# Top-k attention feeding two feed-forward layers: scores as float32 matmuls of 64 rows, the mask by a parametric relu, the gate by tanh, and one form of probabilities for all batches

## The chip, the core and the metric

The kernel runs on one core of a Trainium2 chip. The metric is the device time of one execution in microseconds; the kernel before takes 1081.91 us (median of three runs). The core has a matrix engine (PE, TensorE; PEld is its loading of the stationary operand), a vector engine (DVE), a scalar engine (ACT), a general engine (POOL) and a queue that starts DMA transfers (SP). Each engine works through its own list of instructions in order and waits at semaphores for the others.

## What is computed

Attention over 4 batches of 8 heads, 576 positions and 64 values a head, in which each row of scores keeps its 32 largest entries; its output, as 2304 rows of 512, goes through a gated layer (512 to 1536 to 512) and a layer with a softmax-weighted unit and a layer norm (512 to 1024 to 512).

```python
scores = scale * np.matmul(q, k.transpose(0, 1, 3, 2))
kth = np.partition(scores, -top_k, axis=-1)[..., -top_k:-top_k + 1]
scores = np.where(scores >= kth, scores, -1000000000.0)
attn = np.exp(scores - np.max(scores, axis=-1, keepdims=True))
attn = attn / (np.sum(attn, axis=-1, keepdims=True) + 1e-09)
x = np.matmul(attn, v)                      # then rows of 512
x = (1.0 / (1.0 + np.exp(-(x @ w_gate))) * (x @ w_val)) @ w_out
h = x @ w_in
solu = h * softmax(h)
ln = (solu - mean(solu)) / np.sqrt(var(solu) + 1e-06) * g_ln
return ln @ w_out2
```

## The kernel before

**Steps and chunks.** The attention runs in 72 steps. A step takes 128 query rows of two heads: 64 steps take a block of 128 queries and one pair of heads, eight take the last 64 queries of two pairs, stacked to 128 rows. Four steps fill a chunk of 128 output rows; there are 18 chunks, and each goes through the two layers a few steps after its attention.

**Scores of a step.** `split_k` (L606) and `rest_k` (L610) turn k of a head into a rounded half in partitions 0 to 63 and its rest in 64 to 127; `split_q` (L591) and `rest_q` (L595) do the same with q, which lies in both halves of the partitions. `scores` (L640) sums over 128 rows at once, two matmuls for each half of the 576 keys, in the format float32r. The PSUM tile `ps` has one buffer and holds the scores of one head, so a step goes through it twice: `take_scores` (ACT, L647) copies them to `s`, and `fold_max` and `fold_min` (DVE, L654 and L658) write the larger and the smaller of the two halves into `w`.

**Top 32.** Four rounds on DVE, `topk_max` (L668) with `topk_drop` (L672) in between, the first two over 288 columns and the rest over 576, give the eight largest at a time in `m8`.

**Mask and softmax.** `edge` and `edge_scale` (DVE, L686 and L690) make a scale from the 32nd value, `edge_bias` (POOL, L695 and L696) the bias; `below` (ACT, L701) takes a relu into `w`, which is zero for what stays and huge for what goes; `penal` (POOL, L705) subtracts it from `s`; `expo` (ACT, L710) takes the exponential and its sum; `total1` (POOL) and `inverse` (DVE, L719) give the factor.

**Probabilities.** In batch 0 (`WHOLE`) the row is scaled in float32 by `norm`, transposed on PE (`flip`, L736), copied from PSUM (`take_flip`, L743) and multiplied with float32 values. In the other batches the row becomes two float16 halves (`prob_hi` L749 on ACT, `norm` with one row on ACT at L725 and one on POOL at L727, `prob_lo` L753 on POOL), a DMA transposes them (L760), and `attend` (L779) takes three products of halves. `value_hi` and `value_lo` split v likewise.

**The layers.** `gate` and `value` (L934), `down` (L980), `hidden` (L1017) and `last` (L1115) run three products of float16 halves each. `sigmoid` (L959) takes the gate's twelve blocks in three instructions, after the twelfth; sigmoid and exponential lie in different function tables of ACT, so that a table load stands ahead of each change between them.

**Order.** `Order` is a planner written in Python that runs when the kernel is built. Each operation has an engine, a price in us, a rank, what it needs and which buffers it takes and gives back; the planner plays the five lists forward and emits the instructions in that order. `SHIFT` holds several hundred corrections to the ranks, and `BUFS` the number of buffers of each kind.

Of the kernel before, what the change touches and what calls it, by code (L numbers as in the profile page):

```python
# [43 lines left out]
FULL = 2.0 ** 15  # L44

BUFS = dict(s=3, ks=8, v=4, qr=3, qs=3, w=3, et=2, ps=1, pt=1, av=1, pm=4, xt=1, gh=1, two=3, big=2, xf=1, x2=1)
# [9 lines left out]
EARLY = 6  # L56

# [1201 lines left out]
```

## Time and profile before

| | |
|---|---|
| device time, median of three runs | 1081.91 us (1080.01 to 1081.96) |
| span of the profiled execution | 1076.0 us |
| PE busy | 921.8 us |
| DVE busy | 919.2 us |
| ACT busy | 857.1 us |
| POOL busy | 773.6 us |
| mean granted clock of PE, as a share of full speed | 0.952 |

A busy time is the union of an engine's instructions. Matmuls overlap in the pipeline, so the length of one says little; what a group of them takes is read from its start to the start of the next. The first 150 us bring in and split the weights; from then on attention and layers run side by side until the last steps, and the last 60 us belong to the layers alone.

### The profile page before, as it was taken

What the parts mean: (1) busy time and instruction counts of PE and PEld (TensorE: products, weight loads), DVE (VectorE), ACT (ScalarE), POOL (GpSimd) and SP (SyncE); (2) the same over time, 40 slices, a digit from 0 to 9 for tenths busy, and PEclk for the clock granted to TensorE, in tenths of its full rate; (3) what the DMA queues carried; (4) which work ended last, traced back from release to release, by engine and by line L of the source; (5) the groups of instructions that cost most, each with busy time, mean ns of one, the idle gap of its engine ahead of it and who ended that gap; (6) DMA issues with size and microseconds to landing.
All of it is one profiled execution on the core that took longest, in us unless ns stands there. A gap on an engine that the chain in (4) does not pass through costs nothing.

```text
span 1076.0 us, 30481 instructions
## 1 busy us (share of the span) xinstructions
PE 921.8 (86%) x12014; PEld 752.3 (70%) x12014; DVE 919.2 (85%) x2752; ACT 857.1 (80%) x1535; POOL 773.6 (72%) x970
## 2 busy tenths in 40 slices
PE   2326478899999699999898979998899999999986
PEld 1124377588887678786777877887778788877862
DVE  7999899999697899979899899996898998996232
ACT  4999998887889887977889787877799788886331
POOL 6996867867878977878787867777778777676000
PEclk9997589799999899999899989999999999999988
DMA  9861430001231525244442422335432334143000
GB/s 340 318 221 51 161 122 17 10 17 53 78 97 23 90 36 93 50 93 111 100 90 55 87 61 50 72 71 131 114 83 61 61 70 83 27 75 56 24 11 20
DMA packets 155616, 90.97 MB, mean 85 GB/s; under 512 B 130128, under 2 KB 140368, under 8 KB 155472
## 3 DMA queue, kind: packets, MB, share of 16 engines
q1 hardware_dynamic: 155472, 89.02, 33.6%
q8 instruction: 94, 1.54, 0.6%
q14 instruction: 50, 0.41, 0.1%
HBM read 52.43 MB, written 4.72 MB: 53 GB/s over the span
## 4 chain that ended last, share of the span: by engine, by line
DVE 28%; PE 28%; ACT 17%; POOL 14%; DMA 9%; issue 5%; SPq 0%; POOLq 0%; ACTq 0%; DVEq 0%
DVE m L668 9%; DVE w L672 7%; PE pv L934 5%; PE ph L1017 5%; PE po L1115 4%; DMA kr<-in_k_dup_dram 4%; PE px L980 4%; PE pg L934 3%; POOL s L705 3%; POOL h L753 3%; PE ps L640 2%; ACT w L701 2%; ACT s L710 2%; DVE w L654 2%; DVE w L658 2%
## 5 line engine op out<-in xcount | busy, mean ns | idle before, releaser
L668 DVE MAX8 m<-w 128x8 f32<-128x576 f32 (+1 forms) x576 | 338.4, 601 | 3.0
L672 DVE MATCH_REPLACE8 w<-m,w 128x288 f32<-128x288 f32 (+1 forms) x432 | 233.7, 542 | 0.0
L705 POOL TENSOR_TENSOR s<-s,w 128x576 f32<-128x576 f32 x144 | 203.7, 1419 | 35.0 <-ACT w L701 33.8
L640 PE MATMUL ps<-ks,qs 128*128 128x288 f32 x640 | 130.9, 334 | 53.2 <-DVE w L658 29.8
L980 PE MATMUL px<-gh,wo 128*128 128x128 f16 x2592 | 173.6, 219 | 1.7 <-POOL gh L968 1.7
L980 PEld LDWEIGHTS <-wo 128*128 128x128 f16 x2592 | 153.8, 98 | 26.8 <-issue 2.5
L934 PE MATMUL pg<-xt,wg 128*128 128x128 f16 x2592 | 168.4, 223 | 3.7 <-DVE xt L816 1.5
L934 PE MATMUL pv<-xt,wv 128*128 128x128 f16 x2592 | 165.8, 220 | 1.5 <-ACT sg L959 1.4
L934 PEld LDWEIGHTS <-wv 128*128 128x128 f16 x2592 | 153.7, 99 | 18.6 <-issue 1.6
L934 PEld LDWEIGHTS <-wg 128*128 128x128 f16 x2592 | 154.8, 101 | 8.9 <-issue 5.1
L753 POOL TENSOR_TENSOR h<-s,h 128x576 f16<-128x576 f32 x108 | 139.1, 1291 | 24.5 <-ACT s L725 12.0
L640 PEld LDWEIGHTS ps<-ks,qs 128*128 128x128 f32 x640 | 98.4, 204 | 71.4 <-issue 16.9
L701 ACT ACTIVATE w<-s,ed 128x576 f32<-128x576 f32 x144 | 119.8, 863 | 30.0 <-POOL ed L696 29.6
L1017 PE MATMUL ph<-wi,x 128*128 128x512 f16 x432 | 122.8, 395 | 3.6 <-ACT x L997 2.8
L1115 PE MATMUL po<-wo,lt 128*128 128x512 f16 x432 | 119.2, 391 | 1.1 <-ACT lt L1094 0.6
L710 ACT ACTIVATE s<-s,nm 128x576 f32<-128x576 f32 x144 | 110.9, 771 | 10.7 <-POOL s L705 10.1
L647 ACT ACTIVATE s<-ps 128x576 f32<-128x576 f32 x144 | 92.1, 640 | 23.6 <-PE ps L640 22.7
L654 DVE TENSOR_TENSOR w<-ps,s 128x288 f32<-128x288 f32 x144 | 64.6, 449 | 39.9 <-ACT s L647 26.6
L749 ACT ACTIVATE h<-s,sm 128x576 f16<-128x576 f32 x108 | 82.3, 767 | 16.4 <-DVE sm L719 9.0
L779 PE MATMUL av<-et,v 128*64 128x128 f16 (+3 forms) x2200 | 85.5, 232 | 2.5 <-POOL v L630 1.2
L727 POOL TENSOR_SCALAR s<-s,sm 128x576 f32<-128x576 f32 x78 | 59.1, 760 | 16.1 <-ACT h L749 10.6
L595 POOL TENSOR_TENSOR qs<-qr,qs 128x256 fp32r<-128x256 f32 x80 | 58.6, 733 | 11.0 <-ACT qs L591 10.3
(182 smaller groups left out, 1628.3 us busy)
## 6 DMA issues: line engine op xcount, KB each, us to landing
kr<-in_k_dup_dram SPq DMA_DIRECT2D x16, 576.0 KB, 4.1
qr<-in_q_main_dram SPq DMA_DIRECT2D x64, 128.0 KB, 2.6
v<-in_v_pad_dram SPq DMA_DIRECT2D x16, 320.0 KB, 3.7
wi<-in_w_gate_dram SPq DMA_DIRECT2D x8, 512.0 KB, 6.3
wo<-in_w_val_dram SPq DMA_DIRECT2D x8, 512.0 KB, 8.5
wi<-in_w_out_dram SPq DMA_DIRECT2D x8, 512.0 KB, 5.1
raw<-in_w_in_dram SPq DMA_DIRECT2D x8, 512.0 KB, 3.6
raw<-in_w_out_dram SPq DMA_DIRECT2D x8, 512.0 KB, 3.7
```

Source lines behind the costliest of these rows:

```text
L640: nc.tensor.matmul(pt[:, nn, :S // 2], qs[:, hl, slot], ks[:, nn * (S // 2):(nn + 1) * (S // 2)], start=x == 0, stop=x == len(mm) - 1)
L647: nc.scalar.activation(st["s"][:, t].rearrange("p (a b) -> p a b", a=2), st["ps", t][:, :, :S // 2], AF.Copy)
L668: nc.vector.max(st["m8"][:, t, r * 8:r * 8 + 8], ranked(i, r, t))
L672: nc.vector.match_replace(w, steps[i]["m8"][:, t, r * 8:r * 8 + 8], w, LOW)
L701: nc.scalar.activation(st["w"][:, t], st["s"][:, t], AF.Relu, bias=st["ed"][:, 1, t:t + 1], scale=st["ed"][:, 0, t:t + 1])
L705: nc.gpsimd.tensor_sub(st["s"][:, t], st["s"][:, t], st["w"][:, t])
L710: nc.scalar.activation(w, w, AF.Exp, bias=st["nm"][:, t:t + 1], scale=D ** -0.5, accum_out=st["sm"][:, t:t + 1])
L753: nc.gpsimd.tensor_sub(st["h"][:, 1, t], st["s"][:, t], st["h"][:, 0, t])
L934: nc.tensor.matmul(dst, w[a][:, c, f * P:(f + 1) * P], ch["xt"][:, b, c], start=x == 0, stop=x == len(mm) - 1)
L980: nc.tensor.matmul(ch["px"][:, e], wo1h[a][:, f, e * P:(e + 1) * P], ch["gh"][:, b, f], start=y == 0, stop=y == len(DOWN) - 1)
L1017: nc.tensor.matmul(ch["ph", nn], ch["x2"][:, a, c], wih[b][:, c, nn * 512:(nn + 1) * 512], start=c == 0 and a == 0 and b == 0, stop=c == K ...
L1115: nc.tensor.matmul(ch["po"], ch["lt"][:, a, f], wo2h[b][:, f], start=y == 0, stop=y == len(FIN) - 1)
```

## The change

- **Scores.** `split_q`, `rest_q`, `split_k` and `rest_k` go. k of a pair lies once in float32, one head in partitions 0 to 63 and the other in 64 to 127, and q of a chunk likewise; `scores` multiplies 64 rows of each head, two heads in the two halves of the array, each into a PSUM bank of its own, and the two stacked pairs of the eight short steps also into the two halves of the columns. A pass of `ps` now holds half of the keys of both heads, so that one `fold_max` and one `fold_min` of 2x288 columns do a step.
- **Mask.** `edge`, `edge_scale`, `edge_bias` and `penal` go. `neg_kth` and `span` (POOL, two columns each) make the biases, and `below` is a parametric relu in place on `s`: of the score less the 32nd value, what is negative is multiplied by 3e38.
- **Probabilities.** Batch 0 takes the float16 halves and the DMA's transpose as the others do; `flip` and `take_flip` go, and both rows of `norm` are on POOL.
- **Gate.** `squash` takes tanh of half the argument, one block of four as soon as it is there, and `gated` multiplies (tanh + 1) with the value; the powers of two move into the scales. Tanh, exponential and parametric relu lie in one table: one load is left of 37.
- **Plan.** `BUFS`, prices and the whole of `SHIFT` are new. The plan prices half of a step's scores at 0.5 us, where it had 0.61 and, for the short steps, 1.13.

```diff
-BUFS = dict(s=3, ks=8, v=4, qr=3, qs=3, w=3, et=2, ps=1, pt=1, av=1, pm=4, xt=1, gh=1, two=3, big=2, xf=1, x2=1)
+BUFS = dict(s=4, ks=5, v=4, q=2, w=4, et=2, ps=1, pt=1, av=1, pm=4, xt=1, gh=1, two=3, big=2, xf=1, x2=1)
...
-    ("w", "g"): -1286.9, ("sw", "g"): -576.8, ("wx", "g"): 60.5, ("swx", "g"): 94.2, ("wl", "g"): -67.5,
+    ("w", "g"): -850.7, ("sw", "g"): -415.1, ("wx", "g"): -364.4, ("swx", "g"): 350.7, ("wl", "g"): -67.5,
...
-        nc.gpsimd.tensor_sub(qs[:, 1], qr, qs[:, 0].bitcast(F32))
...
-        nc.gpsimd.tensor_sub(ks[D:], kr[D:], ks[D:].bitcast(F32))
+        kv["k", b, p] = kt = tl(sp, [P, S], F32, f"k{b}_{p}", "ks")
+        for t in range(2):
+            nc.sync.dma_start(kt[t * D:t * D + D], k_dup[b, 2 * p + t, t * D:t * D + D])
...
-                nc.tensor.matmul(pt[:, nn, :S // 2], qs[:, hl, slot], ks[:, nn * (S // 2):(nn + 1) * (S // 2)],
-                                 start=x == 0, stop=x == len(mm) - 1)
...
+        for x, p in enumerate(st["pairs"]):
+            for t in range(2):
+                rows = slice(t * D, t * D + D)
+                if st["rem"]:
+                    cols = slice(x * REM, x * REM + REM)
+                    nc.tensor.matmul(ps[cols, t, :S // 2], q[rows, 2 * st["c"] + x, cols], kv["k", b, p][rows, keys],
+                                     start=True, stop=True)
+                else:
+                    nc.tensor.matmul(ps[:, t, :S // 2], q[rows, p], kv["k", b, p][rows, keys], start=True, stop=True)
...
+        nc.vector.tensor_tensor(st["w"][:, :, :S // 2], st["ps", 1][:, :, :S // 2], st["s"][:, :, :S // 2], op=OP.max)
...
-        nc.scalar.activation(st["w"][:, t], st["s"][:, t], AF.Relu, bias=st["ed"][:, 1, t:t + 1], scale=st["ed"][:, 0, t:t + 1])
-
-    def penal(i, t):
-        st = steps[i]
-        nc.gpsimd.tensor_sub(st["s"][:, t], st["s"][:, t], st["w"][:, t])
+        w = st["s"][:, t]
+        nc.scalar.activation(w, w, AF.Prelu, bias=st["nk"][:, t:t + 1], alpha=PICK)
...
-            nc.scalar.activation(ch["sg", f], ch["pg", f], AF.Sigmoid, scale=factors[ch["key"]])
+    def squash(ch, f):
+        ch["sg", f] = tl(sp, [P, 4, P], F32, "sg", "two")
+        nc.scalar.activation(ch["sg", f], ch["pg", f], AF.Tanh, scale=factors[ch["key"]])
...
+            add(("qk", i, n), "PE", 0.5, t0 - STEP, lambda i=i, n=n: scores(i, n),
```

POOL around the mask of step 40 (`s40`, `ed40`, `nk40` and so on belong to that step, `h39` are the halves of the step ahead, `qs44` is a later step's q), before:

```order
L695 TENSOR_TENSOR ed40_9430<-m840_9257,ed40_9430 128x2
L696 TENSOR_SCALAR ed40_9430<-ed40_9430 128x2
L678 TENSOR_SCALAR nm40_9500<-m840_9257 128x2
L595 TENSOR_TENSOR qs44_0_9442<-qr44_0_8754,qs44_0_9442 128x256
L705 TENSOR_TENSOR s40_9108<-s40_9108,w40_9180 128x576
L753 TENSOR_TENSOR h39_9534<-s39_8862,h39_9534 128x576
L727 TENSOR_SCALAR s39_8862<-s39_8862,sm39_9106 128x576
L705 TENSOR_TENSOR s40_9108<-s40_9108,w40_9180 128x576
```

and with the change:

```order
L693 TENSOR_SCALAR s39_8345<-s39_8345,sm39_8733 128x576 x2
L705 TENSOR_TENSOR h39_8888<-s39_8345,h39_8888 128x576
L662 TENSOR_SCALAR nk40_8966<-m840_8641 128x2
L705 TENSOR_TENSOR h39_8888<-s39_8345,h39_8888 128x576
L668 TENSOR_TENSOR nb40_9025<-m840_8641 128x2
L669 TENSOR_SCALAR nb40_9025<-nb40_9025 128x2
```

The two subtractions over 576 columns between relu and exponential, and the rest of q, are gone from POOL; a second scaling of the row has come, and the biases of step 40 stand between the halves of step 39.

DVE at the first maxima of step 40 (`w40` are its folded scores, `m840` its maxima), before:

```order
L668 MAX m840_9257<-w40_9180 128x8
L672 MATCH_REPLACE w40_9180<-m840_9257,w40_9180 128x288
L654 TENSOR_TENSOR w40_9180<-ps40_1_9263,s40_9108 128x288
L372 TENSOR_SCALAR n2_9288<-ptot_9307 128x1
L668 MAX m840_9257<-w40_9180 128x8
```

and with the change:

```order
L639 TENSOR_TENSOR w40_8610<-ps40_1_8574,s40_8515 128x2x288
L688 RECIPROCAL sm38_8554<-sm38_8554 128x2
L653 MAX m839_8424<-w39_8410 128x8
L653 MAX m840_8641<-w40_8610 128x8 x2
L653 MAX m839_8424<-w39_8410 128x8
L643 TENSOR_TENSOR w40_8610<-ps40_1_8574,s40_8515 128x2x288
```

Before, the second head's fold stood behind the first head's first round; now one fold serves both heads, ahead of both first rounds, and the last rounds of step 39 stand among them.

## Rows read from the trace of the kernel before

**Rows 1.** The page's busy times: us, share of the span, instructions.

```profile
PE 921.8 (86%) x12014; PEld 752.3 (70%) x12014; DVE 919.2 (85%) x2752; ACT 857.1 (80%) x1535; POOL 773.6 (72%) x970
```

**Rows 2.** Windows: us; busy (count) of PE, PEld, DVE, ACT, POOL; PE clock, DMA, GB/s.

```profile
900.00:1000.00 100.00, 98.89 (x1435) 81.77 (x1434) 85.75 (x258) 73.09 (x130) 65.48 (x85) 1.00 0.34 62
```

**Rows 3.** The page's chain that ended last, share of the span by engine.

```profile
DVE 28%; PE 28%; ACT 17%; POOL 14%; DMA 9%; issue 5%; SPq 0%; POOLq 0%; ACTq 0%; DVEq 0%
```

**Rows 4.** The gate's line, L959: count; ns min/median/max; first and last start, us; forms.

```profile
L959 ACT ACTIVATE sg<-pg,fs_x x48: 678/687/692, 154.2 to 1012.7; 128x512 f32<-128x512 f32 x48
L959 ACT ACT_TABLE_LOAD  x18: 1283/1283/1283, 152.9 to 1010.3; - x18
```

**Rows 5.** PE in time, 406 to 411: start us, us, line, operands, count.

```profile
406.18 0.84 PE L1017 MATMUL ph<-wi,x 128*128 128x512 f16 x3
406.85 0.84 PE L1115 MATMUL po<-wo,lt 128*128 128x512 f16 x3
407.62 1.03 PE L779 MATMUL av<-et,v 128*64 128x128 f16 x30
408.58 1.51 PE L980 MATMUL px<-gh,wo 128*128 128x128 f16 x24
409.91 0.77 PE L640 MATMUL ps<-ks,qs 128*128 128x288 f32 x4
410.52 0.23 PE L934 MATMUL pg<-xt,wg 128*128 128x128 f16 x1
```

**Rows 6.** PE in time, 221 to 224, in batch 0.

```profile
221.75 0.61 PE L736 MATMUL pt<-ident,s 128*128 128x128 f32 x4
222.29 1.31 PE L779 MATMUL av<-et,v 128*64 128x128 f32 x20
223.53 0.68 PE L934 MATMUL pg<-xt,wg 128*128 128x128 f16 x9
```

**Rows 7.** PE in time, 308 to 310, half of a short step's scores.

```profile
308.78 1.30 PE L640 MATMUL ps<-ks,qs 128*128 128x288 f32 x8
309.92 0.85 PE L980 MATMUL px<-gh,wo 128*128 128x128 f16 x12
```

**Rows 8.** DVE in time, 507 to 510.

```profile
507.38 0.13 DVE L690 TENSOR_SCALAR ed<-ed 128x1 uint32<-128x1 uint32 x1
507.44 0.09 DVE L672 MATCH_VALUE_LOAD w<-m,w 128x8 f32 x1
...
508.77 0.75 DVE L668 MAX8 m<-w 128x8 f32<-128x576 f32 x1
509.44 0.44 DVE L654 TENSOR_TENSOR w<-ps,s 128x288 f32<-128x288 f32 x1
509.80 0.14 DVE L686 TENSOR_SCALAR ed<-m 128x1 uint32<-128x1 uint32 x1
```

**Rows 9.** Groups by line: count, busy us, mean ns, idle before and its enders.

```profile
L705 POOL TENSOR_TENSOR s<-s,w 128x576 f32<-128x576 f32 x144 | 203.7, 1419 | 35.0 <-ACT w L701 33.8 <-DVE w L658 0.5
L753 POOL TENSOR_TENSOR h<-s,h 128x576 f16<-128x576 f32 x108 | 139.1, 1291 | 24.5 <-ACT s L725 12.0 <-DVE m L668 3.9 <-issue 2.2
L701 ACT ACTIVATE w<-s,ed 128x576 f32<-128x576 f32 x144 | 119.8, 863 | 30.0 <-POOL ed L696 29.6
L710 ACT ACTIVATE s<-s,nm 128x576 f32<-128x576 f32 x144 | 110.9, 771 | 10.7 <-POOL s L705 10.1
L749 ACT ACTIVATE h<-s,sm 128x576 f16<-128x576 f32 x108 | 82.3, 767 | 16.4 <-DVE sm L719 9.0 <-DVE ed L690 2.4 <-DMA et<-h 2.3
L727 POOL TENSOR_SCALAR s<-s,sm 128x576 f32<-128x576 f32 x78 | 59.1, 760 | 16.1 <-ACT h L749 10.6 <-DVE sm L719 3.0 <-DVE ed L686 1.3
L595 POOL TENSOR_TENSOR qs<-qr,qs 128x256 fp32r<-128x256 f32 x80 | 58.6, 733 | 11.0 <-ACT qs L591 10.3
L610 POOL TENSOR_TENSOR ks<-kr,ks 64x576 fp32r<-64x576 f32 x32 | 45.1, 1414 | 10.1 <-ACT ks L606 8.6
```

**Rows 10.** DMA issues: line, count, median us from issue to landing.

```profile
et<-h SPq DMA_TRANSPOSE x54, 5.1
```

More of the change, by code (lines that the diff above doesn't have):

```diff
@@ L176 @@
                 POOL=(100, 70, 80, 100, 1250), DMA=(0,) * 5)
-    TAKER = dict(s="ACT", ks="POOL", v="DMA", qr="DMA", qs="POOL", w="DVE", et="ACT", ps="PE", pt="PE", av="PE", pm="PE",
+    TAKER = dict(s="ACT", ks="DMA", v="DMA", q="DMA", w="DVE", et="DMA", ps="PE", pt="PE", av="PE", pm="PE",
                  xt="ACT", gh="ACT", two="ACT", big="DMA", xf="ACT", x2="ACT")
@@ L384, in over_partitions @@
     def over_partitions(col):
-        pt = tl(pp, [P, 3, P], F32, "ptot", "pt")
+        pt = tl(pp, [P, 512], F32, "ptot", "pt")
         num = col.shape[-1]
-        nc.tensor.matmul(pt[:, 0, 0:num], ones, col, start=True, stop=True)
-        return pt[:, 0, 0:num]
+        nc.tensor.matmul(pt[:, 0:num], ones, col, start=True, stop=True)
+        return pt[:, 0:num]
     ncol = npiece = 0
@@ L561, in mains @@
             for c in range(NMAIN):
-                ch = dict(rows=[(b * S + c * P, P)], key=f"x{b}", vs=(b,))
+                ch = dict(rows=[(b * S + c * P, P)], key=f"x{b}", vs=(b,), rem=False, c=c)
                 chunks.append(ch)
                 for p in range(NPAIR):
-                    steps.append(dict(ch=ch, b=b, rem=False, c=c, pairs=(p,), first=p == 0, last=p == NPAIR - 1, o=0))
+                    steps.append(dict(ch=ch, b=b, rem=False, c=c, pairs=(p,), first=p == 0, last=p == NPAIR - 1, o=0, j=0))
         mains(b2)
-        ch = dict(rows=[((b2 + j) * S + NMAIN * P, REM) for j in range(2)], key=f"y{b2}", vs=(b2, b2 + 1))
+        ch = dict(rows=[((b2 + j) * S + NMAIN * P, REM) for j in range(2)], key=f"y{b2}", vs=(b2, b2 + 1), rem=True)
         chunks.append(ch)
@@ L571, in body @@
                 steps.append(dict(ch=ch, b=b2 + j, rem=True, c=h, pairs=(2 * h, 2 * h + 1),
-                                  first=j == 0 and h == 0, last=j == 1 and h == 1, o=j * REM))
+                                  first=j == 0 and h == 0, last=j == 1 and h == 1, o=j * REM, j=j))
         mains(b2 + 1)
@@ L630, in value_lo, with scores @@
         nc.gpsimd.tensor_sub(lo, kv["ts", b, p, x], hi)
-    def scores(i, t):
+    def scores(i, n):
         st = steps[i]
-        b, qs = st["b"], st["qs", t if st["rem"] else 0]
-        st["ps", t] = pt = tl(pp, [P, 2, 512], F32, f"ps{i}_{t}", "ps")
-        terms = [(x if st["rem"] else t, kv[b, p, t]) for x, p in enumerate(st["pairs"])]
-        mm = [(hl, slot, ks) for slot, ks in terms for hl in range(2)]
-        for x, (hl, slot, ks) in enumerate(mm):
-            for nn in range(2):
-                nc.tensor.matmul(pt[:, nn, :S // 2], qs[:, hl, slot], ks[:, nn * (S // 2):(nn + 1) * (S // 2)],
-                                 start=x == 0, stop=x == len(mm) - 1)
@@ L643, in take_scores @@
-    def take_scores(i, t):
+        b = st["b"]
+        st["ps", n] = ps = tl(pp, [P, 2, 512], F32, f"ps{i}_{n}", "ps")
+        q = st["ch"]["q", st["j"]]
+        keys = slice(n * (S // 2), (n + 1) * (S // 2))
+        for x, p in enumerate(st["pairs"]):
+            for t in range(2):
+                rows = slice(t * D, t * D + D)
+                if st["rem"]:
+                    cols = slice(x * REM, x * REM + REM)
+                    nc.tensor.matmul(ps[cols, t, :S // 2], q[rows, 2 * st["c"] + x, cols], kv["k", b, p][rows, keys],
+                                     start=True, stop=True)
+                else:
+                    nc.tensor.matmul(ps[:, t, :S // 2], q[rows, p], kv["k", b, p][rows, keys], start=True, stop=True)
@@ L723, in norm @@
         w = st["s"][:, t]
[L724 to L727 removed]
+        nc.gpsimd.tensor_scalar(w, w, st["sm"][:, t:t + 1], 1.0, op0=OP.mult, op1=OP.mult)
     BLOCKS = [0, 5, 1, 6, 2, 7, 3, 8, 4]
[L731 to L743 removed]
     def prob_hi(i, t):
@@ L800, in row_factors @@
             yield (slice(x * n, x * n + n),
-                   scale[ch["key"]][0] if b in WHOLE else 1.0 / PROB if own else factors["row", ch["key"], b])
+                   1.0 / PROB if own else factors["row", ch["key"], b])
     def scaled_rows(ch, dst):
@@ L830, in body @@
         t = use[0] * STEP
-        add(("kd", b, p), "DMA", 1.64, t - 3 * STEP, lambda b=b, p=p: load_k(b, p),
-            [("qk", uses[b - 1, p][-1], j) for j in range(2)] if b else [], take=["s"], delay=0.95,
-            room=lambda b=b, p=p: room_k(b, p))
-        for j in range(2):
-            add(("kb", b, p, j), "ACT", 0.57, t - 2 * STEP,
-                lambda b=b, p=p, j=j: split_k(b, p, j), [("kd", b, p)], take=["ks"])
-            add(("ka", b, p, j), "POOL", 1.36, t - 2 * STEP, lambda b=b, p=p, j=j: rest_k(b, p, j),
-                [("kb", b, p, j)] + [("ka", b, p, 0)] * j, free=["s"] * j)
+        add(("kd", b, p), "DMA", 1.0, t - 3 * STEP, lambda b=b, p=p: load_k(b, p),
+            ([("kd", b, p - 1)] if p else [("kd", b - 1, NPAIR - 1)] if b else []), take=["ks"], delay=0.95)
         add(("vd", b, p), "DMA", 0.91, t - STEP, lambda b=b, p=p: load_v(b, p), take=["v"], delay=0.95)
         add(("vn", b, p), "ACT", 0.75, t + STEP, lambda b=b, p=p: norm_v(b, p), [("vd", b, p)], take=["xf"], free=["xf"])
-        for x in range(0 if b in WHOLE else 2):
+        for x in range(2):
             add(("vh", b, p, x), "ACT", 0.9, t + STEP, lambda b=b, p=p, x=x: value_hi(b, p, x), [("vn", b, p), ("ve", f"x{b}")],
@@ L844, in body @@
             add(("vl", b, p, x), "POOL", 0.75, t + STEP, lambda b=b, p=p, x=x: value_lo(b, p, x), [("vh", b, p, x)], free=["two"])
+    for x, ch in enumerate(chunks):
+        ch["steps"] = [i for i, st in enumerate(steps) if st["ch"] is ch]
+        for j in range(len(ch["vs"])):
+            add(("qd", x, j), "DMA", 0.8, ch["steps"][2 * j] * STEP - 3 * STEP, lambda ch=ch, j=j: load_q(ch, j),
+                [("qd", x, j - 1) if j else ("qd", x - 1, len(chunks[x - 1]["vs"]) - 1)] if x or j else [], take=["q"], delay=0.95)
     for i, st in enumerate(steps):
@@ L848, in body @@
         rem, b, ch = st["rem"], st["b"], st["ch"]
-        for t in range(2 if rem else 1):
-            add(("qd", i, t), "DMA", 0.47, t0 - 3 * STEP, lambda i=i, t=t: load_q(i, t), take=["qr"], delay=0.95)
-            add(("qb", i, t), "ACT", 0.31, t0 - 2 * STEP,
-                lambda i=i, t=t: split_q(i, t), [("qd", i, t)], take=["qs"])
-            add(("qa", i, t), "POOL", 0.7, t0 - 2 * STEP, lambda i=i, t=t: rest_q(i, t), [("qb", i, t)], free=["qr"])
-        for t in range(2):
-            add(("qk", i, t), "PE", 1.13 if rem else 0.61, t0 - STEP, lambda i=i, t=t: scores(i, t),
-                [("qa", i, t if rem else 0)] + [("ka", b, p, t) for p in st["pairs"]], take=["ps"],
-                free=(["qs"] if rem or t == 1 else []) + ["ks"] * sum(uses[b, p][-1] == i for p in st["pairs"]))
-            add(("se", i, t), "ACT", 0.53, t0 - STEP, lambda i=i, t=t: take_scores(i, t), [("qk", i, t)] + [("se", i, 0)] * t,
-                take=["s"] * (t == 0))
+        done_q = st["last"] or rem and ch["steps"].index(i) == 1
@@ new lines, in body @@
+        for n in range(2):
+            add(("qk", i, n), "PE", 0.5, t0 - STEP, lambda i=i, n=n: scores(i, n),
+                [("qd", ch["x"], st["j"])] + [("kd", b, p) for p in st["pairs"]] + ([("qk", i, 0)] if n else [("qk", i - 1, 1)] if i else []), take=["ps"],
+                free=(["q"] * done_q + ["ks"] * sum(uses[b, p][-1] == i for p in st["pairs"])) * n)
+            add(("se", i, n), "ACT", 0.53, t0 - STEP, lambda i=i, n=n: take_scores(i, n), [("qk", i, n)] + [("se", i, 0)] * n,
+                take=["s"] * (n == 0), free=["ps"] * (n == 0))
@@ L871, in body @@
                 cost = (0.36 if r < 2 else 0.664) if kind == "m" else (0.43 if r < 2 else 0.727)
-                add((kind, i, r, t), "DVE", cost, t0 + 0.8 * x, lambda fn=fn, i=i, r=r, t=t: fn(i, r, t), needs)
-        add(("nm", i), "POOL", 0.17, t0, lambda i=i: neg_max(i), [("m", i, 0, 0), ("m", i, 0, 1)])
+                add((kind, i, r, t), "DVE", cost, t0 + 0.8 * x, lambda fn=fn, i=i, r=r, t=t: fn(i, r, t), needs,
+                    free=["w"] * ((kind, r, t) == ("m", 3, 1)))
+        add(("nk", i), "POOL", 0.17, t0 + 0.8 * len(chain), lambda i=i: neg_kth(i), [("m", i, 3, 0), ("m", i, 3, 1)])
@@ L874, in body @@
+        add(("nb", i), "POOL", 0.34, e, lambda i=i: span(i), [("nk", i)])
         for t in range(2):
-            order.seq(("es", i, t), "DVE", [(0.07, lambda i=i, t=t: edge(i, t)), (0.1, lambda i=i, t=t: edge_scale(i, t))],
-                      t0 + 0.8 * len(chain), [("m", i, TOPK // 8 - 1, t)])
-        add(("eb", i), "POOL", 0.435, e, lambda i=i: edge_bias(i), [("es", i, 0), ("es", i, 1)])
-        for t in range(2):
-            add(("be", i, t), "ACT", 0.76, e, lambda i=i, t=t: below(i, t), [("eb", i)])
-            add(("pe", i, t), "POOL", 1.385, e, lambda i=i, t=t: penal(i, t), [("be", i, t)] + [("pe", i, 0)] * t, free=["w"] * t)
-            add(("ex", i, t), "ACT", 0.76, e, lambda i=i, t=t: expo(i, t), [("pe", i, t), ("nm", i)], table="exp")
+            add(("be", i, t), "ACT", 0.76, e, lambda i=i, t=t: below(i, t), [("nk", i), ("se", i, 1)])
+            add(("ex", i, t), "ACT", 0.76, e, lambda i=i, t=t: expo(i, t), [("be", i, t), ("nb", i)])
@@ L902, in body @@
-        needs = [("et", i, x) for x in range(3)] if whole else [("tr", i)]
-        needs += [n for p in st["pairs"] for n in ([("vd", b, p)] if whole else [("vl", b, p, x) for x in range(2)])]
+        for t in range(2):
+            add(("hh", i, t), "ACT", 0.67, e, lambda i=i, t=t: prob_hi(i, t), [("iv", i)] + [("hh", i, 0)] * t, take=["w"] * (t == 0))
+            add(("no", i, t), "POOL", 0.73, e, lambda i=i, t=t: norm(i, t), [("hh", i, t)])
+            add(("hl", i, t), "POOL", 1.385, e, lambda i=i, t=t: prob_lo(i, t), [("no", i, t)] + [("hl", i, 0)] * t,
+                free=["s"] * t)
@@ L904, in body @@
+        add(("tr", i), "DMA", 3.5, e + 3, lambda i=i: flip_halves(i), [("hl", i, 1)], take=["et"], free=["w"], delay=1.5,
+            room=lambda i=i: room_halves(i))
+        needs = [("tr", i)] + [("vl", b, p, x) for p in st["pairs"] for x in range(2)]
         needs += [("at", i - 1)] * (i > 0 and not st["first"])
-        add(("at", i), "PE", 1.41 if whole else 1.18 if rem else 1.06, e + 6, lambda i=i: attend(i), needs,
+        add(("at", i), "PE", 1.18 if rem else 1.06, e + 6, lambda i=i: attend(i), needs,
@@ L917, in body @@
             for bb in ch["vs"]:
-                if bb not in WHOLE and key != f"x{bb}":
+                if key != f"x{bb}":
                     add(("vk", key, bb), "DVE", 0.2, e, lambda key=key, bb=bb: row_scale(key, bb), [("ve", key), ("ve", f"x{bb}")])
@@ L1022, in start @@
         def start():
[L1023 removed]
+            ch["st"] = sp.tile([P, 10], F32, name="st", tag="st", bufs=5)
             part(0)
@@ L1146, in body @@
                take=["pm"] if f % 4 == 0 else [])
-        op(("sg",), "ACT", 1.75, 12, lambda ch=ch: sigmoid(ch), [("ga", x, f) for f in range(KF1)] + [("fs", key)],
-           take=["two"] * 3 + ["gh"], free=["pm"] * 3, table="sig")
+        for y, f in enumerate((8, 0, 4)):
+            op(("sg", f), "ACT", 0.58, 12, lambda ch=ch, f=f: squash(ch, f), [("ga", x, f + 3), ("fs", key)] + done["v"] * (x == 0),
+               take=["two"], free=["pm"])
         for y, f in enumerate((8, 9, 10, 11, 0, 1, 2, 3, 4, 5, 6, 7)):
             op(("va", f), "PE", 0.687, 12 + y + (y > 9), lambda ch=ch, f=f: value(ch, f),
-               [("xl", x)] + done["v"] * (x == 0) + [("va", x, f - 1)] * (f % 4 > 0) + [("ga", x, f) for f in (3, 7, 11)] +
+               [("xl", x)] + done["v"] * (x == 0) + [("va", x, f - 1)] * (f % 4 > 0) + [("ga", x, f + 3)] * (f % 4 == 0) +
                [("va", x, 3), ("va", x, 11)] * (f == 7),
```

191 lines of the change are left out of this document (63 added, 128 removed), and 137 rows, old and new, of the table SHIFT.

## The prediction, made before the changed kernel ran

> **What bounds the kernel now.** I read the busy times first [rows 1]: PE and DVE stand level at 86 and 85%, ACT and POOL not far below, so no engine bounds the kernel alone. The chain of waits says the same [rows 3]: PE and DVE hold 28% each, but ACT, POOL and DMA together 40%. The end is set by PE and DVE work with the helpers' latency in between. In a good stretch PE is 98.9% busy at full clock [rows 2], the best that the rest can be brought to.
>
> For a sum I need the pace. The gate's nonlinearity runs once a chunk; its first start is at 154.2 and its last at 1012.7 [rows 4], so 17 intervals of 50.5 us lie between, a lead-in of 154.2 ahead, and 1076.0 - 1012.7 = 63.3 behind. Against 50.5 I set PE's work for a chunk, priced from start to start at full clock. Groups of twelve 128-column matmuls take 0.665 (24 in 1.33), groups of three 512-column ones 0.67 [rows 5]; there are 648 and 288: 431 + 193. Half of a step's scores takes 0.61 [rows 5], in the eight short steps 1.14 [rows 7]: 128 and 16 of them, 96. An `attend` takes 0.96 with halves [rows 5] and 1.24 in float32 [rows 6]: 54 and 18, 74. Four transposes take 0.54, of which 0.10 belongs to the change of array layout discussed below, so 0.11 each [rows 6]: 162 for probabilities and 144 in the layers, 18 + 16. Together 828, or 46.0 a chunk: PE fills **91%** of the interval.
>
> **The change, part by part.** *PE without the scores.* The 162 transposes go (-17.8) and 18 float32 attends become halves (18 x 0.28 = -5.0): 828 - 96 - 23 leaves 709.
>
> *The scores, the term that decides.* The trace of before has no matmul on half of the rows. The nearest row is the float32 `attend` [rows 6]: ten float32 matmuls of 128 columns, recorded as twenty, in the two column halves of the array. Without 0.10 for leaving that layout they take 1.14, or 0.228 a pair, a little over the 0.213 that four passes of 128 columns take at 2.4 GHz; so two run at a time, each with four passes. For 288 columns four passes are 0.48. If the two heads run side by side in the row halves, half of a step takes 0.48, and the short steps' four quarters the same. Whether a change of layout costs anything has a row too: three 512-column matmuls ahead of an `attend` take 0.77 and not 0.67 [rows 5], so 0.10 on the way in; I take the same on the way out. Then it is 0.68 against 0.61 now, and 0.68 against 1.14. For 144 halves: 69 at the low end (no cost of layout), **98** by the nearest row, which I take, and 182 at the high end, where the heads run one after the other (1.16 for 128 halves, 2.12 for 16). PE per chunk is then 43.2, **44.8** or 49.5.
>
> The Trainium skill (TensorEngine Tiling (Array Packing), Key Properties) says that a change of the tiling mode, not of the tile, drains the engine; it speaks against this change, which makes 288 such changes more. The 0.10 of the row agrees with it, and by the rule it holds for row halves as well: 98 rather than 69, or 1025 rather than 996 us at the end.
>
> *DVE.* 288 one-column operations go; one costs 0.06 start to start [rows 8], 17 us. Four folds of 0.36 become two of twice the width; the nearest row of that width is a MAX8 at 0.67 [rows 8]: 1.44 against 1.34, 7 us over 72 steps. 919 falls to 895, less than PE gains or loses.
>
> *POOL.* `penal` 203.7, the rest of q 58.6 and of k 45.1 go; 36 more `prob_lo` at 1.291 (46), 66 more scalings at 0.760 (50) and eight halves of v (under 10) come [rows 9]: 774 becomes about 573. The two-column operations stay as many.
>
> *ACT.* 36 table loads at 1.283 [rows 4] and 66 scalings at about 0.77 go, 36 `prob_hi` at 0.767 come [rows 9]: -69; 16 roundings of v at most +12; the 112 roundings of q and k and the 54 copies out of PSUM come off that at no more than 0.77 each. Parametric relu: between the exponential with one column operand, 771, and today's relu with two, 863 [rows 9]; I take 771, as it has one. ACT falls from 857 to 800 at most.
>
> *What that frees.* None of the helpers' time is on PE or DVE, so it is worth only what PE stops waiting. Of a step's mask, two 1.4 us subtractions leave the path from the 32nd value to the probabilities, and k no longer passes ACT and POOL. I let PE's filling rise from 91 to **95%**, the middle between now and the 99% of [rows 2]. Late next is then PE itself, with DVE (895 of some 1020, 88%) close behind.
>
> *What batch 0 pays.* Its 18 steps wait for a DMA transpose that lands 5.1 us after its issue [rows 10] and for v, split after all four pairs are read. On the SP queue these transposes stand ahead of the late weight loads, which wait for each. The lead-in I leave at 154.2, with 10 us either way for the range; the tail is unchanged.
>
> *Sum.* 44.8 / 0.95 = 47.2 a chunk; 17 x 47.2 = 802; with 154.2 and 63.3 a span of 1019. The median of the runs lies 5.9 above the profiled span (1081.9 against 1076.0): **1025 us**.
>
> **The rivals.**
> - *The heads run one after the other*, and the kernel is slower. Place: the two matmuls of a half step. Price: 1.16 a half, PE 49.5 a chunk, at 95% 52.1, so 886 + 217.5 + 5.9 = 1109. It decides once a half of a main step takes over 0.9 or so without better filling elsewhere. Against it: in [rows 6] float32 pairs do run two at a time. For it: that row has column halves, and no row has row halves.
> - *The pair runs staggered.* Each float32 matmul has two records; if the second head's first must wait for the first head's second to start, a half takes 1.5 x 0.48 + 0.20 = 0.92 (short steps 1.40), scores 140, PE 47.2, at 95% 49.7: 1068. For it: the two records of a matmul. Against: 0.228 a pair leaves no room for it in a run of ten. The Trainium skill (TensorE: Matmul & The Clock Gate, Part 3) has matmuls start strictly in program order, which would give this result; no row here decides it for a lone pair.
> - *The helpers were not what PE waited for*, and DVE, which loses only 24 us, sets the pace. Filling stays 91%: 44.8 / 0.91 = 49.2, 837, so 1060. For it: DVE's share of the chain [rows 3]; one buffer of `ps` still ties PE, ACT and DVE in turn, as the second half waits for the copy of the first and the fold for the second. Against: two passes of `ps` with DVE in each become one.
> - *No cost of layout at all*: 43.2, at 95% 45.5, 773, so 996.
>
> **How the numbers follow.** Forecast 1025: 0.46 (own range 1008 to 1042, from filling 93 to 97%). Staggered 1068: 0.10. Pace of DVE 1060: 0.16. No layout cost 996: 0.16. Serial 1109: 0.12. The range that leaves out the serial case and little else is 985 to 1072: the low end is 996 less the 10 us of the lead-in, the high end just holds the staggered pair. Faster by over 0.2%, about the least that a measurement of this kernel tells from no change: all but the serial case, less a little for two misses at once, 0.86; within 0.2%: 0.02; slower: 0.12.
>
> **What would show it.** In the changed trace: half of a main step's scores 0.6 to 0.7 from start to start, and the short steps' no longer (0.5: no layout cost; 0.9: staggered; 1.16: serial). Gate intervals of about 47, with first start near 154. POOL's busy time near 573, ACT's below 800, DVE's near 895. The forecast is wrong if scores take over 0.9, if intervals stay near 49 while PE shows gaps that end at DVE, or if the first gate comes later than 165.

## The result

The changed kernel takes **1001.99 us** (median of four runs, 1001.85 to 1002.34) against 1081.38 for the kernel before: a ratio of 0.928, 95% interval 0.9257 to 0.9304. The forecast was 1025, in a range of 985 to 1072. Its profiled execution has a span of 1000.6 us, so the 75.4 us between the two spans (1076.0 before) are what has to be explained. The medians lie 79.4 apart; the other 4 are there because the execution profiled before was faster than its median (a run takes 1.7 to 1.8 us more than its span, so that one took 1077.8).

The first answer comes from the page of the changed kernel: the busy times, and the chain of waits by engine (before: [rows 1, 3]).

```profile
PE 883.0 (88%) x12052; PEld 668.1 (67%) x12052; DVE 865.0 (86%) x2321; ACT 724.4 (72%) x1319; POOL 569.6 (57%) x824
...
PE 75%; DVE 13%; ACT 6%; DMA 3%; issue 1%; POOL 1%; SPq 0%; POOLq 0%; ACTq 0%; DVEq 0%
```

PE's part of the chain rises from 28 to 75%, that of POOL and DMA falls from 23 to 4%. The chain no longer passes from engine to engine; it is PE's own work. The windows of the middle of the run say the same (us; busy with count of PE, PEld, DVE, ACT, POOL; PE clock, DMA share, GB/s), first in the kernel before:

```profile
300.00:800.00 500.00, 463.17 (x6464) 385.83 (x6463) 445.94 (x1396) 417.51 (x759) 390.92 (x503) 0.97 0.38 79
```

and in the changed kernel:

```profile
300.00:800.00 500.00, 499.43 (x7009) 374.71 (x7007) 476.20 (x1320) 383.28 (x720) 294.95 (x458) 1.00 0.35 76
```

Before, no engine was busy for more than 93% of these 500 us. After, PE is busy for 499.4 of them, DVE for 476, and the helpers are well below. The gate's line gives the pace, as in [rows 4]: count, ns, first and last start.

```profile
L886 ACT ACTIVATE sg<-pg,fs_x x48: 662/687/705, 158.6 to 947.6; 128x512 f32<-128x512 f32 x48
```

There is no table load in it any more. 17 intervals lie between 158.6 and 947.6, so **46.4 us a chunk** against 50.5. The 75.4 us are then 69.5 of pace (17 x 4.1), 10.3 of tail (1000.6 - 947.6 = 53.0 against 63.3), less 4.4 of a later first gate.

The scores come next, the term that was to decide. PE in time in the changed kernel (start us, us, line, operands, count), around half of a main step:

```profile
561.16 0.83 PE L909 MATMUL px<-gh,wo 128*128 128x128 f16 x12
561.92 0.76 PE L628 MATMUL ps<-k,q 64*128 64x288 f32 x4
562.61 0.84 PE L909 MATMUL px<-gh,wo 128*128 128x128 f16 x12
563.29 0.83 PE L863 MATMUL pg<-xt,wg 128*128 128x128 f16 x12
```

From its start to the next start the half takes 0.69. Twelve fp16 matmuls take 0.68 when others of the same layout follow (562.61 to 563.29), and 0.76 ahead of the scores (561.16 to 561.92): so the way into the layout lies outside the 0.69 and comes to 0.08 or 0.09 more. A short step's half, in the same view:

```profile
267.49 0.71 PE L625 MATMUL ps<-k,q 64*64 64x288 f32 x8
268.13 0.85 PE L946 MATMUL ph<-wi,x 128*128 128x512 f16 x3
```

0.64, where it took 1.14 before [rows 7]. Last, the groups of the mask and the folds (count, busy us, mean ns, idle before and what ended it), to be set beside [rows 8, 9]:

```profile
L675 ACT ACTIVATE s<-s,nk 128x576 f32<-128x576 f32 x144 | 105.3, 767 | 32.5 <-POOL nk L662 32.3
...
L705 POOL TENSOR_TENSOR h<-s,h 128x576 f16<-128x576 f32 x144 | 184.5, 1285 | 3.1 <-POOL nk L662 0.2
...
L639 DVE TENSOR_TENSOR w<-ps,s 128x576 f32<-128x576 f32 x72 | 54.1, 751 | 26.1 <-ACT s L634 17.5 <-PE ps L628 4.5 <-ACT lt L1023 1.8
...
L643 DVE TENSOR_TENSOR w<-ps,s 128x576 f32<-128x576 f32 x72 | 53.6, 744 | 0.1
```

The parametric relu takes 767 ns where 771 was taken, and the relu with two column operands took 863.

### The profile page after: what moved, and what is told of

It is laid out like the page before. It is cut to its first block, busy times and chain, and to the rows that moved or that the text cites. A ratio compares the mean times of both kernels' runs of the same rounds, so it can differ in the third digit from the quotient of the medians.

```text
span 1000.6 us, 29578 instructions
## 1 busy us (share of the span) xinstructions
PE 883.0 (88%) x12052; PEld 668.1 (67%) x12052; DVE 865.0 (86%) x2321; ACT 724.4 (72%) x1319; POOL 569.6 (57%) x824
## 4 chain that ended last, share of the span: by engine, by line
PE 75%; DVE 13%; ACT 6%; DMA 3%; issue 1%; POOL 1%; SPq 0%; POOLq 0%; ACTq 0%; DVEq 0%
PE pg L863 15%; PE pv L863 14%; PE px L909 12%; PE ph L946 9%; PE po L1044 9%; PE ps L628 8%; PE av L727 6%; DVE m L653 3%; DVE w L657 2%; PE pl L1018 2%; DVE pd L424 1%; DMA raw<-in_w_in_dram 1%; DMA wi<-in_w_gate_dram 1%; DVE pd L427 1%; PE ps L625 1%
## 5 line engine op out<-in xcount | busy, mean ns | idle before, releaser
L653 DVE MAX8 m<-w 128x8 f32<-128x288 f32 (+1 forms) x576 | 328.6, 598 | 0.1
L705 POOL TENSOR_TENSOR h<-s,h 128x576 f16<-128x576 f32 x144 | 184.5, 1285 | 3.1 <-POOL nk L662 0.2
L693 POOL TENSOR_SCALAR s<-s,sm 128x576 f32<-128x576 f32 x144 | 106.7, 745 | 102.2 <-ACT h L701 101.7
L628 PE MATMUL ps<-k,q 64*128 64x288 f32 x512 | 105.3, 488 | 28.9 <-ACT s L634 11.7
L675 ACT ACTIVATE s<-s,nk 128x576 f32<-128x576 f32 x144 | 105.3, 767 | 32.5 <-POOL nk L662 32.3
L701 ACT ACTIVATE h<-s,sm 128x576 f16<-128x576 f32 x144 | 107.4, 767 | 20.4 <-DVE sm L688 16.6
L680 ACT ACTIVATE s<-s,nb 128x576 f32<-128x576 f32 x144 | 110.0, 766 | 1.1 <-POOL nb L669 1.0
L628 PEld LDWEIGHTS ps<-k,q 64*128 64x128 f32 x512 | 42.1, 198 | 67.8 <-issue 21.4
L727 PE MATMUL av<-et,v 128*64 128x128 f16 (+1 forms) x2400 | 77.9, 220 | 6.5 <-ACT v L608 6.0
L727 PEld LDWEIGHTS <-v 128*64 128x64 f16 x2400 | 66.3, 113 | 23.9 <-issue 12.7
L639 DVE TENSOR_TENSOR w<-ps,s 128x576 f32<-128x576 f32 x72 | 54.1, 751 | 26.1 <-ACT s L634 17.5
L684 POOL TENSOR_SCALAR sm<-sm 128x2 f32<-128x2 f32 x72 | 13.8, 191 | 108.9 <-ACT s L680 103.7
```

What stands on the lines that cost most here:

```text
L628: nc.tensor.matmul(ps[:, t, :S // 2], q[rows, p], kv["k", b, p][rows, keys], start=True, stop=True)
L653: nc.vector.max(st["m8"][:, t, r * 8:r * 8 + 8], ranked(i, r, t))
L680: nc.scalar.activation(w, w, AF.Exp, bias=st["nb"][:, t:t + 1], scale=D ** -0.5, accum_out=st["sm"][:, t:t + 1])
L693: nc.gpsimd.tensor_scalar(w, w, st["sm"][:, t:t + 1], 1.0, op0=OP.mult, op1=OP.mult)
L701: nc.scalar.activation(st["h"][:, 0, t], st["s"][:, t], AF.Copy, scale=st["sm"][:, t:t + 1])
L705: nc.gpsimd.tensor_sub(st["h"][:, 1, t], st["s"][:, t], st["h"][:, 0, t])
```

## The experiments

My theory after the result: the changed kernel runs at PE's pace, and the gain is PE being kept at work, not PE having less of it. The rivals: DVE's lighter load set the new pace; PE's work was the pace on both sides; the new table of numbers, which orders the work, made the gain. Each run is compared by its ratio to runs of the kernel before on the same chip; where a difference to the changed kernel is given, it is the difference of the two ratios times 1080 us. By their intervals the gains and losses below are uncertain by 2 to 4 us each.

**Is the pair side by side, and does PE's time pass on?** Both heads are put on the same rows:

```
-  nc.tensor.matmul(ps[:, t, :S // 2], q[rows, p], kv["k", b, p][rows, keys], ...)
+  nc.tensor.matmul(ps[:, t, :S // 2], q[:D, p], kv["k", b, p][:D, keys], ...)
```

(and the short steps' line in the same way)

> The changed kernel with one edit: the second head of a pair is scored from the rows of the first head, so both matmuls of a half step sit on the same half of the array's rows and can only follow each other (the second head's scores are not its own here; shapes, buffers and the order of the instructions stay). If the pair runs side by side in the changed kernel and PE sets its pace: a half of a main step takes 1.1 to 1.25 from start to start instead of 0.69, 128 x 0.47 = 60 us more, the 16 short halves 0.5 to 1.5 more each, so 1068 to 1086 us in all. If the pair ran one after the other already: no change, 1002. If it runs side by side but DVE or the helpers set the pace: half steps as above, but the time under 1030.

1066.67 us, ratio 0.9862 (0.9841 to 0.9883): 63 us more than the changed kernel. PE in time:

```profile
561.61 1.23 PE L628 MATMUL ps<-k,q 64*128 64x288 f32 x4
562.78 0.84 PE L863 MATMUL pv<-xt,wv 128*128 128x128 f16 x12
```

A half takes 1.17 instead of 0.69, 0.48 more; the short halves 0.48 more too, since their quarters still run two at a time in the column halves. 144 x 0.48 = 69 us of PE work gave 63 us of time, a little under the range I wrote down, in which short steps stood as dearer. So the pair does run side by side in the changed kernel, this is worth 63 us of the kernel's time, and most of what PE has more to do is seen at the end.

**PE's work less, in the changed kernel and in the kernel before.** One of the gate's three products is left out in both:

```
-  mm = [(c, a, b) for c in range(KD) for a, b in TERMS]
+  mm = [(c, a, b) for c in range(KD) for a, b in (TERMS[:2] if w is wgh else TERMS)]
```

> The changed kernel without the third of the gate's three products (the low half of its weights against the high half of the rows is left out): 48 matmuls of 128 columns a chunk, 864 in all, 864 x 0.055 = 48 us of PE work less; every wait, buffer and other instruction stays. If PE sets the pace from 200 us on: 954 to 964 us. If DVE does (865 us busy): 990 or more. If the helpers' latency does: between, 970 to 990.

> The kernel before with the same edit (the third product of the gate left out, 48 us of PE work less). If PE was short of work for 9% of each interval because DVE, the copies and the one score buffer held it up: 15 to 35 us less, 1047 to 1066. If PE set the pace there as fully as in the changed kernel: 45 to 48 less, 1034 to 1037.

The changed kernel: 974.09 us, ratio 0.9013 (0.8996 to 0.9029), 29 us less for 48 us of work (45 by PE's busy time, 883.0 to 838.4). The kernel before: 1078.32 us, ratio 0.9982 (0.9963 to 1.0), 2 us less for the same 48. In the changed kernel less work, the middle reads:

```profile
300.00:800.00 500.00, 489.37 (x6750) 360.88 (x6748) 489.36 (x1366) 389.59 (x739) 302.30 (x476) 1.00 0.35 78
```

PE and DVE now stand level at 98%. I take DVE, now as full as PE, for the reason that 29 came and not 48; PE's own waits in this stretch, 10.6 us, don't single it out, as the longest sums are 2.1 us behind POOL and 2.0 behind ACT. In the kernel before less work:

```profile
300.00:800.00 500.00, 445.39 (x5936) 365.33 (x5933) 442.87 (x1391) 415.01 (x757) 388.94 (x501) 0.94 0.37 79
```

PE's busy time just fell, from 463 to 445, and the gate's intervals stayed at 50.5:

```profile
L959 ACT ACTIVATE sg<-pg,fs_x x48: 677/687/692, 155.9 to 1015.2; 128x512 f32<-128x512 f32 x48
```

Over the whole run PE's busy time fell by 31 (921.8 to 890.5) and not by 48, because PE's granted clock fell too (0.97 to 0.94 in these 500 us); even the 31 moved the end by only 2. No expectation for this kernel held; each allowed PE too much. For the changed kernel 974 fell where I had put the helpers' latency, while the window points at DVE. **PE's work was worth next to nothing in the kernel before.** That also ends the rival by which the gain came through PE's work.

**DVE's work more in the changed kernel, less in the kernel before.** The last MAX8 of a step's first head is done twice in the changed kernel; in the kernel before one MATCH_REPLACE of a step is left out:

```
+  for _ in range(2 if (r, t) == (TOPK // 8 - 1, 0) else 1):
       nc.vector.max(st["m8"][:, t, r * 8:r * 8 + 8], ranked(i, r, t))
```

```
+  if (r, t) != (2, 0):
       nc.vector.match_replace(w, steps[i]["m8"][:, t, r * 8:r * 8 + 8], w, LOW)
```

> The changed kernel with the last MAX8 of a step's first head done twice (same result): 72 x 0.66 = 48 us more on DVE, and 0.66 more ahead of each step's mask. If PE sets the pace and DVE has slack: 1000 to 1012 us. If DVE's relief is what the gain came from: 1040 to 1050.

> The kernel before without one of the six MATCH_REPLACEs of a step (the third of the first head is left out, so that its last eight values repeat the eight ahead of them): 72 x 0.73 = 52 us of DVE work less, the order of the rest stays. If DVE with its waits is the pace of the kernel before, where PE's 48 us were worth 2: 35 to 50 us less, 1030 to 1045. If the pace is the latency of ACT, POOL and the transposes: 10 to 25 less. If DVE has slack as PE has: within 5.

The changed kernel with 48 us more on DVE: 1031.92 us, ratio 0.9551 (0.9533 to 0.957), 29 us more, between the two expectations. In the middle PE falls to 486 of 500 and DVE rises to 490:

```profile
300.00:800.00 500.00, 486.38 (x6865) 366.18 (x6863) 490.06 (x1326) 371.59 (x705) 288.17 (x449) 1.00 0.33 75
```

So PE sets the pace of the changed kernel, but DVE stands close behind it: my theory gave DVE too much slack.

The kernel before with 52 us less on DVE (44 by its busy time, 919.2 to 875.3): 1075.00 us, ratio 0.9957 (0.9939 to 0.9975), 5 us less, the case in which DVE has slack as PE has. DVE's waits there (us in total, times, longest):

```profile
DVE w L654 <- ACT s L647: 21.9, 24, 3.9
DVE sm L720 <- POOL sm L716: 10.3, 14, 2.0
```

DVE's longest waits in the kernel before as it was, in the same 500 us:

```profile
DVE w L654 <- ACT s L647: 13.8, 10, 3.9
DVE w L654 <- DMA et<-h: 10.8, 5, 4.2
...
DVE sm L719 <- POOL sm L715: 4.3, 3, 2.2
```

The two waits grew from 13.8 to 21.9 and from 4.3 to 10.3: 14 of the 23 us that DVE saved in this stretch (its busy time fell from 446 to 423) turned into waits for ACT and POOL. With PE's result this says that the pace of the kernel before was not the work of PE and not that of DVE. That it was the ring through all engines is my reading: it fits the longest waits in 300 to 800, in which each engine waits for another, and the next runs test two of its links.

```profile
ACT w L701 <- POOL ed L696: 21.8, 11, 5.3
POOL s L705 <- ACT w L701: 21.0, 19, 2.8
POOL sm L715 <- ACT s L710: 19.8, 15, 2.2
PE ps L640 <- DVE w L658: 16.6, 9, 4.9
```

**Each part alone, in the kernel before.** First the mask; the edge operations, the relu into `w` and the subtractions go, the order of what is left stays:

```
-  nc.scalar.activation(st["w"][:, t], st["s"][:, t], AF.Relu, bias=..., scale=...)
...
-  nc.gpsimd.tensor_sub(st["s"][:, t], st["s"][:, t], st["w"][:, t])
+  w = st["s"][:, t]
+  nc.scalar.activation(w, w, AF.Prelu, bias=st["nk"][:, t:t + 1], alpha=PICK)
```

> The kernel before with the mask alone by a parametric relu in place (no edge operations, no relu into a second buffer, no subtractions of 204 us on POOL); all else, and the order of what is left, stays. Taking 48 us of PE's work away from the kernel before moved it by only 2 us, so PE's work is not its pace. If its pace is the ring of a step (scores copied by ACT, folded and sorted on DVE, masked by ACT and POOL, buffers free again): the mask is a long link of the ring, 15 to 40 us less. If DVE's own work is the pace: only the 288 one-column operations count, 10 to 17 us less. If neither, within 3 us.

1065.73 us, ratio 0.9876 (0.985 to 0.9903): 13 us less for 200 us less on POOL. That is a little under what I gave the ring, and in the range of DVE's own work; but since 52 us of DVE's work were worth 5, the 17 us that I had put on the edge operations can't be it.

The tanh gate, the order kept:

```
-  nc.scalar.activation(ch["sg", f], ch["pg", f], AF.Sigmoid, scale=...)
+  nc.scalar.activation(ch["sg", f], ch["pg", f], AF.Tanh, scale=...)
```

(with the factor 0.5 and the `(tanh + 1) x value` of the change)

> The kernel before with the gate alone by tanh: the 36 later table loads of 1.28 us go (46 us on ACT), all else, and the order of the instructions, stays. If ACT's share of the ring counts: 8 to 25 us less, since some of the loads stand in front of exponentials or copies that DVE waits for. If PE or DVE alone is the pace: within 4 us.

1066.07 us, ratio 0.9885 (0.986 to 0.9909): 12 us less for 46 us of table loads.

Both of these together:

> The kernel before with the new mask and the tanh together, the order of what is left kept. Alone they gave 13.4 and 12.4 us. If they add up: 24 to 28 less, 1052 to 1056. If they help each other (ACT waits for POOL and DVE for ACT): over 32 less. If the order, made for the old costs, or PE is what comes next: under 20.

1060.27 us, ratio 0.9825 (0.9802 to 0.9848): 19 us, less than the 26 of the two apart: under the old order the two reliefs overlap. The page's chain of this kernel suggests what comes next:

```profile
PE 49%; DVE 6%; ACT 5%; DMA 3%; POOL 2%; issue 1%; POOLq 0%; DVEq 0%; ACTq 0%
```

POOL and ACT, 31% of the chain in [rows 3], are down to 7%, and PE holds 49 of the 66% that the shares sum to (this chain was followed back over two thirds of the span only, that of [rows 3] over all of it).

Scores and halves, with the functions of the changed kernel for `load_q`, `load_k`, `scores` and the folds, `WHOLE = ()`, and four buffers of `s` and `w`:

> The kernel before with the native float32 scores, two heads side by side (and with them one fold of double width in place of two, no splitting of q and k on ACT and POOL, four buffers each of s and w in the room that they leave) and with all batches' probabilities as float16 halves; mask and gate as before; the planner sets the order anew with the numbers of the kernel before. If the ring is the pace: 20 to 50 us less, as buffers and helpers come free. If the gain of the whole change came through PE's work (23 us less in these two parts): 15 to 23 less. If the numbers that set the order outweigh both: no gain or a loss.

1071.30 us, ratio 0.9925 (0.9897 to 0.9952): 8 us less. That is under what either mechanism would give, and not the missing gain of the third case, so no case held. The gate's line tells more:

```profile
L941 ACT ACTIVATE sg<-pg,fs_x x48: 677/687/705, 165.1 to 1007.5; 128x512 f32<-128x512 f32 x48
```

That is 49.6 us a chunk, 16 us less than before over 17 intervals, but the first gate comes 11 us later than before (165.1 against 154.2). The order here was made anew from numbers that were not made for it; that this is why the start is late was not tested, and the 16 do not tell the two mechanisms apart.

So the parts gave 13, 12 and 8 us, 34 together, or 27 if the mask and the tanh are counted as they ran together. The whole change gave 78. By pace alone (17 intervals of the gate) it was 13, 11 and 16, together 41, of the 69.5.

**The order's table, and the buffers.** The table `SHIFT` is left empty in both kernels:

> The changed kernel with the table of numbers that shifts the planner's order left empty, so that the planner orders by its own costs and due times alone. To be set against the kernel before with its table left empty too. Each part alone gained 8 to 13 us in the kernel before, 34 together, where the whole change gained 78. If the other 44 come from the parts' working together: both kernels lose alike, and the ratio of the two stays at 0.92 to 0.94. If they come from the new table: this kernel loses 40 us more than the other does, and the ratio is 0.96 to 0.97.

> The kernel before with its table of numbers left empty, the other half of the comparison: 1090 to 1170 us, and the changed kernel's share of it 0.92 to 0.94 if the parts work together, 0.96 to 0.97 if the new table made the rest.

Without it the changed kernel takes 1048.63 us (ratio 0.9724, 0.9705 to 0.9743) and the kernel before 1120.52 (1.041, 1.0374 to 1.0446). Both lose alike, 48 and 44 us, and the ratio of the two is 0.9724 / 1.041 = 0.934, which is 71 us on 1080. **The gain is mainly the parts' and not the table's**: of 78 us some 7 hang on the new numbers. That is the balance of larger items, as the gate's line shows, first of the kernel before and then of the changed kernel, both with the empty table:

```profile
L888 ACT ACTIVATE sg<-pg,fs_x x48: 678/687/695, 137.5 to 1064.1; 128x512 f32<-128x512 f32 x48
L816 ACT ACTIVATE sg<-pg,fs_x x48: 664/682/691, 125.1 to 994.0; 128x512 f32<-128x512 f32 x48
```

The pace falls from 54.5 to 51.1, which is 58 us over 17 intervals against 69.5 with the tables; the first gate comes 12 us earlier instead of 4 later, and the tail (spans 1117.8 and 1045.3) gains 2 us instead of 10. So the new numbers add to the pace and to the tail, and lose about as much in the lead-in.

Then the changed kernel with three buffers of `s` and `w`:

```
-  BUFS = dict(s=4, ks=5, v=4, q=2, w=4, ...
+  BUFS = dict(s=3, ks=5, v=4, q=2, w=3, ...
```

> The changed kernel with three buffers each of s and w, as many as before, instead of four; the planner sets the order anew. If the buffers are what closes the ring: DVE waits for copies and for w again and falls from 95 to 90% in the middle of the run, 1025 to 1060 us. If PE sets the pace with room to spare: 1000 to 1008.

1015.33 us, ratio 0.9416 (0.9392 to 0.944): 15 us more, between the two expectations. PE stays busy for 496 of the 500 us:

```profile
300.00:800.00 500.00, 496.36 (x6971) 375.46 (x6972) 455.94 (x1266) 373.94 (x704) 286.11 (x445) 1.00 0.34 73
```

The fourth buffers, in the room that the split q and k left, are worth 15 us here, with an order that the planner made anew without numbers for it; they don't make or break the new pace, which is 47.0 us a chunk without them and 46.4 with them. What stays open is which parts together make up the difference between 34 and 71: of the pairs only mask and tanh were run together, the changed kernel was not run with one part taken back, and every part alone ran under an order made for the old work, or one made from the old numbers.

## Why the prediction was right, step by step

The direction and the range held, and so did the scores side by side. The form of the sum did not, and that 1025 came as near as it did is in part luck, since two errors in it went opposite ways. The 23 us between 1025 and 1002 are 13 of pace (802 against 789), 10 of tail, less 4 of lead-in, and some 4 in what is added to the span: the forecast added 5.9, the median lies 1.4 above the profiled span. Of the 5.9 only 1.8 lie around a span; the rest was that the execution profiled before was faster than the median.

**Scores: the mechanism right, the size not.** The pair runs side by side, a half takes 0.69 where 0.68 was taken, and serial matmuls cost the 1.17 that the rival had (its short steps, at 2.12 forecast and 1.13 measured, apart). But 0.68 was to hold both changes of layout, and 0.69 holds one: the way in, 0.09, lies in the group ahead. The full cost is 0.78. What I had left out I take for a weight load. Of a half's four records, two start 6 or 7 ns apart, the other two 0.35 after the first, and the next group 0.335 after that; with the heads in a row the records behind the first follow at 0.24. So the first two are 0.11 longer than their passes, and the second load of weights begins 0.107 after the first matmul does; that one makes the other was not tested. The term is then 128 x 0.78 + 16 x 0.74 = 112 and not 98. The same way in was missing at the `attend`s, in both kernels, 6 to 7 us each. PE's work was therefore 46.4 a chunk before and is 45.9 now, not 46.0 and 44.8: **PE gained almost nothing in work.**

**The cost of a change of layout** was right in size: 0.149 from the last record ahead to the first score, where matmuls of the layers follow at 0.056, which is 0.093. The rival without it was wrong by that much. By the Trainium skill (TensorEngine Tiling (Array Packing), Key Properties) changing the tiling mode drains the engine; the trace agrees, for row halves as for column halves, and puts 0.093 us on it. The changed kernel has 405 such changes and the kernel before 142; at this price the 405 are 38 us of PE's work, an estimate.

**The staggered pair** was wrong. Its premise, that the second head's first record must wait for the first head's second, is refuted by the 6 ns. The rule of the Trainium skill behind it (TensorE: Matmul & The Clock Gate, Part 3: matmuls start and end in program order) is not: the first records of the two do start in that order, 6 or 7 ns apart. My step from it to the second records was the error.

**Filling: the step that failed in size.** I let it rise from 91 to 95%, the middle between two values. With the corrected work it was 46.4 / 50.5 = 92% and is 45.9 / 46.4 = 99%. The middle was a guess where the profile gave a reason: the longest sum of PE's waits in the kernel before, 16.6 of the 37 us that it was idle in 300 to 800, ended at DVE's fold of the one score buffer, and the change took something away at that link and at others. The two errors, work too low and filling too low, partly cancelled, which is the luck in 1025.

**Work times filling was the wrong form for the kernel before.** In that kernel 48 us of PE work were worth 2 and 52 us of DVE work under 5. Some 22 of my 56 us of pace (17 x 1.2 / 0.91) were booked on PE's work being less; by the run with less PE work that term is worth near nothing there, and the work hardly fell. The sentence that the helpers' time "is worth only what PE stops waiting" was right: by the corrected sums nearly all of the gain is PE waiting less (of 69.5 us of pace, 17 x 0.5 = 8.5 would be its work).

**DVE as the pace** was wrong as a rival, and its premise with it: relief of the helpers alone, by the mask and by the tanh, gave 13 and 12 us. But it was nearer than its 0.16 says, since DVE stands at 95% in the middle of the run.

**The helpers and DVE.** POOL 573 forecast, 569.6 measured; ACT at most 800, 724.4 measured; DVE 895 forecast, 865.0 measured, mis-sized by 30. Counted from the start of each instruction to the next or to its own end, whichever comes first, the folds fell from 105 to 96 us where I had them fall by 7, so that term was right. The edge operations took 24 where I had 17, as one pair of starts had stood for all. Most of the rest is the four rounds of maxima and replacements, of which there are as many as before: they took 545 and now take 527, and I had no term for that.

**Lead-in and tail.** The first gate came at 158.6, 4.4 late and within the 10 allowed; it starts at 125 in the changed kernel with an empty table, so the order decides it. The tail was not unchanged. It is 53.0 in the changed kernel, 53.7 in the kernel before with an empty table and 51.3 in the changed kernel with one, and 61 to 65 in all variants that keep the old table or its numbers: the 10 us belong to the order and not to any part.

## What to carry to other kernels

Where four engines are all busy 70 to 86% of the time and none is full through the middle of the run, ask first whether an engine's work counts at all: a run with 5% of one engine's work left out tells whether to price the change by work or by links of the ring. In this kernel the reliefs were worth more all together (71 us with empty tables, 78 with the tables) than apart (34), though the one pair that was run together gave less (19 of 26). Once one engine was full its work passed on to the time: 63 of 69 us added, but only 29 of 48 taken out, with the next engine close behind. When a group of matmuls is priced from start to start, what the change of layout costs on the way in stands in the group ahead of it.

## What the hardware showed that I had not expected

PE's granted clock in 300 to 800 was 0.97 before and is 1.00 now. In the kernel before with less PE work it was 0.94: the emptier PE was given the lower of its two levels (1.2 GHz) for 58 of these 500 us, against 27 in the kernel before as it was, which takes back part of the work that it was spared. The full PE of the changed kernel kept 2.4 GHz throughout these 500 us.

Two native float32 matmuls on the two row halves start 6 or 7 ns apart and take 0.69 us, where the two on the same half take 1.17. One alone is then some 0.68, an estimate from the first record's 0.35 and the last one's 0.335. Four quarters, two by rows and two by columns, take 0.64 against 0.69 for the two halves.

The parametric relu with a slope of 3e38 costs what an exponential costs (767 against 766 ns), and stands in one table with it and the tanh: of the table loads one is left in the whole run.
